# A fourth U buffer, transposes ahead of the broadcasts, and the reciprocals' small DMAs on GpSimd's queue, in a fused attention and MoE kernel

## The chip, the cores and the metric

One core of one Trainium2 chip. The metric is device time in microseconds (us). Executions are called fast or slow (a slow one is over 1.5% above the fastest of the same kernel); times below are medians of all runs, and ratios use fast runs alone.

## The reference

```python
# attention: B=8, H=12, S=448, D=64; cap = 30
scores = cap * np.tanh(scale * (q @ k.T) / cap)
attn   = np.exp(scores - max);  attn = attn / (sum(attn) + 1e-09)
out    = attn @ v
# MoE on x = out as (3584, 768); w1, w2: 768 x 1024, w_out: 1024 x 768
g = np.maximum(x @ w1, x @ w2)
y = g @ w_out
```

## The kernel before

Two heads make a pair, two pairs a quad; there are 24 quads, t = 0 to 23, and three pairs make a group g whose k, q and v are loaded together. TensorE computes scores, ScalarE tanh and exp. `pv` multiplies with v and gives U, not yet normalized, and the row sums. A small chain then fetches the reciprocals: the sums are gathered from 4 partitions by a DMA of 7 KB, inverted on VectorE, stored to DRAM (7 KB) and broadcast from there to 64 partitions twice (224 KB each). GpSimd multiplies U by it (`normalize`) into xT, and one MoE block per three quads consumes xT. MoE matmuls are strewn between the attention's, `F(n)` of them at a time, in a fixed order.

```python
def pv(t, ab):
    ...
    if ab == 0:
        U[t] = upool.tile([P, 2, S], f32, name="u", bufs=3)
    nc.vector.tensor_copy(U[t][:, ab, :], ps[:, :S])
    if ab:
        st = upool.tile([P, S], f32, name="st", bufs=1)
        nc.vector.tensor_copy(st, ss[:, :S])
        sums[t] = xpool.tile([32, 56], f32, name="sums")
        nc.sync.dma_start(out=sums[t], in_=st. ...)          # 7 KB
def invert(t):
    nc.vector.reciprocal(r, sums[t])
    nc.sync.dma_start(out=recd[t], in_=r)                    # rec_d, in DRAM, 7 KB
def spread(t):
    for h in range(2):
        nc.sync.dma_start(out=rec[t][64*h : 64*h+64], in_=...to_broadcast(...))   # rec_b
def normalize(t, ab, eng=nc.gpsimd):
    eng.tensor_mul(xT..., U[t][:, ab, :], rec[t][:, ab, :])
...
for t in range(NQ):
    scores(t + 1, 0); ex(t, 3); ...
    if t > 4:
        spread(t - 2)
    extra(i)            # loads, casts on GpSimd, cross(g): crossbar transposes
    ...
    pv(t, 0); ...
    if t > 4:
        normalize(t - 2, 0); normalize(t - 2, 1)
    scores(t + 1, 2); ...
    if t > 4:
        invert(t - 1)
    elif t > 1:
        spread(t - 2)
    extra(i + 1); ...
    pv(t, 1); ...       # ends with the sums' DMA
    if 0 < t < 5:
        invert(t - 1)
    if 1 < t < 5:
        normalize(t - 2, 0); normalize(t - 2, 1)
```

Each engine works through its own list in order; a wait in that list holds everything behind it (the 5.60 us for which VectorE stands in the prediction's first timeline are such a case).

## Time and profile before

| | before |
|---|---|
| time, median of the first 3 runs | 378.1 us (377.25 to 382.38) |
| the profiled execution | 380.94 us, span 379.2 us |
| TensorE, ScalarE, VectorE, GpSimd busy | 92%, 74%, 53%, 40% |

### The profile page before, as it was taken

How to read it: one execution, taken by the hardware profiler on the slowest of the kernel's cores; microseconds unless marked ns; L12 is line 12 of the kernel's file. 1: busy time of each engine (PE TensorE's matmuls, PEld its weight loads, DVE VectorE, ACT ScalarE, POOL GpSimd, SP SyncE). 2: the span in 40 equal slices, each digit the busy share in tenths (PEclk: the TensorE clock that was granted, in tenths of full speed). 3: DMA queues.
4: the chain of work that ended last, by engine and by line, in shares of the span. 5: the costliest groups of instructions: out<-in, count | busy, mean ns of one | idle time of the engine just before them, and what ended most of it. 6: DMA issues, size and time to landing. Idle time of an engine off the chain costs nothing.

```text
span 379.2 us, 6549 instructions
## 1 busy us (share of the span) xinstructions
PE 349.0 (92%) x2492; PEld 168.2 (44%) x2492; DVE 200.6 (53%) x348; ACT 281.8 (74%) x265; POOL 150.1 (40%) x188
## 2 busy tenths in 40 slices
PE   3677986898999999999999999999989999999996
PEld 2223443443444444444444454434434444555563
DVE  4223473567665676455745654557448556633421
ACT  4999986697999989998898899889958897000000
POOL 3734135637554445444562456243644302420000
PEclk9997898999999999999999999999989999999999
DMA  7999999996788987999698959896988132422022
GB/s 251 263 209 220 274 284 223 227 193 139 215 212 221 213 232 203 223 234 255 177 213 208 251 163 250 232 242 165 216 217 213 51 91 105 122 80 95 2 83 84
DMA packets 104464, 71.56 MB, mean 189 GB/s; under 512 B 58224, under 2 KB 99440, under 8 KB 104432
## 3 DMA queue, kind: packets, MB, share of 16 engines
q1 hardware_dynamic: 102480, 67.99, 71.1%
q0 software_dynamic: 1952, 3.15, 4.5%
q8 instruction: 19, 0.31, 0.4%
q14 instruction: 13, 0.11, 0.1%
HBM read 53.48 MB, written 11.18 MB: 171 GB/s over the span
## 4 chain that ended last, share of the span: by engine, by line
PE 65%; DMA 19%; DVE 5%; SPq 4%; ACT 3%; issue 2%; POOL 1%; POOLq 0%; DVEq 0%; ACTq 0%
PE mm L396 17%; PE mm L411 16%; PE mm L408 12%; PE pv L334 6%; DMA qkT<-kqf 6%; PE s L295 6%; DMA qr<-in_q_dram 6%; DMA vr<-in_v_dram 4%; DMA rec_b<-rec_d 3%; PE pv L348 3%; PE ss L347 2%; PE s L290 1%; DVE u L351 1%; ACT expo L303 1%; ACT tanh L296 1%
## 5 line engine op out<-in xcount | busy, mean ns | idle before, releaser
L296 ACT ACTIVATE tanh<-s 128x896 bf16<-128x896 f32 x144 | 124.3, 915 | 32.5 <-PE s L295 31.1
L303 ACT ACTIVATE expo<-tanh 128x1792 bf16<-128x1792 bf16 (+1 forms) x96 | 144.9, 1510 | 0.1
L383 POOL TENSOR_TENSOR xT<-u,rec_b 128x448 bf16<-128x448 f32 x48 | 58.4, 1238 | 101.1 <-DMA rec_b<-rec_d 81.2
L411 PE MATMUL mm<-wo_sb,gT 128*128 128x384 bf16 x448 | 86.8, 330 | 0.0
L396 PE MATMUL mm<-xT,wd_sb 128*128 128x448 bf16 x384 | 79.1, 354 | 2.7 <-POOL xT L383 1.3
L351 DVE COPY u<-pv 128x448 f32<-128x448 f32 x48 | 29.9, 624 | 91.0 <-PE pv L348 78.3
L408 PE MATMUL mm<-wm_sb,xT 128*128 128x384 bf16 x336 | 66.6, 326 | 0.2 <-DVE gT L400 0.2
L411 PEld LDWEIGHTS <-gT 128*128 128x128 bf16 x448 | 43.6, 99 | 31.1 <-issue 3.6
L415 DVE COPY osb<-mm 128x384 f32<-128x384 f32 x56 | 31.1, 555 | 46.3 <-PE mm L411 46.0
L396 PEld LDWEIGHTS <-wd_sb 128*128 128x128 bf16 x384 | 37.2, 98 | 38.4 <-issue 5.9
L295 PE MATMUL s<-qkT 64*128 64x448 bf16 x288 | 43.2, 371 | 11.1 <-ACT tanh L298 3.4
L400 DVE TENSOR_SCALAR gT<-mm 128x448 bf16<-128x448 f32 x64 | 39.1, 616 | 16.8 <-PE mm L396 16.6
L408 PEld LDWEIGHTS <-xT 128*128 128x128 bf16 x336 | 32.5, 98 | 23.3 <-issue 1.9
L334 PE MATMUL pv<-expo,vp 128*64 128x448 bf16 x288 | 37.5, 370 | 0.0
L158 POOL CAST vp<-vr 128x1152 bf16<-128x1152 f32 x15 | 18.0, 1201 | 46.8 <-DMA vr<-in_v_dram 43.5
L321 DVE TENSOR_TENSOR esum<-esum,expo 128x896 bf16<-128x896 bf16 x38 | 29.9, 787 | 1.5
L319 DVE TENSOR_TENSOR esum<-expo 128x896 bf16<-128x896 bf16 x38 | 26.6, 699 | 0.0
L295 PEld LDWEIGHTS <-qkT 64*128 64x128 bf16 x288 | 9.4, 95 | 36.8 <-issue 28.7
L298 ACT ACTIVATE tanh<-s 128x896 bf16<-128x896 f32 x24 | 22.0, 917 | 4.4 <-PE s L290 3.9
L334 PEld LDWEIGHTS <-vp 128*64 128x64 bf16 x288 | 12.4, 110 | 21.3 <-issue 15.2
L232 PE MATMUL mm<-wo_sb,w2T 128*128 128x384 bf16 x96 | 19.1, 334 | 1.4 <-DVE qkT L264 1.4
L178 POOL CAST kqf<-qr 128x1152 bf16<-128x1152 f32 x12 | 14.5, 1207 | 9.6 <-DMA qr<-in_q_dram 9.4
(56 smaller groups left out, 227.7 us busy)
## 6 DMA issues: line engine op xcount, KB each, us to landing
rec_b<-rec_d SPq DMA_DIRECT2D x48, 224.0 KB
kr<-in_k_dram SPq DMA_DIRECT2D x12, 576.0 KB
qr<-in_q_dram SPq DMA_DIRECT2D x12, 576.0 KB
vr<-in_v_dram SPq DMA_DIRECT2D x12, 576.0 KB
out_dram<-osb SPq DMA_DIRECT2D x17, 384.0 KB
out_dram<-osb SPq DMA_DIRECT2D x22, 192.0 KB
osb<-in_moe_w_dram SPq DMA_DIRECT2D x6, 512.0 KB
vr<-in_v_dram SPq DMA_DIRECT2D x8, 288.0 KB
```

The lines of the kernel that those rows point to most:

```text
L295: nc.tensor.matmul(s[:, h, :S], k0[r, j * P : (j + 1) * P], qTn[r, :])
L296: nc.scalar.activation(tanh[t, p][:, 2 * m : 2 * m + 2, :], s[:, :, :S], AF.Tanh, scale=scale / cap)
L303: nc.scalar.activation(expo[t, p], tanh[t, p][:, 0:n, :], AF.Exp, scale=float(cap))
L321: nc.vector.tensor_add(d, d, e_of(t, ab, 0 if ab else 2))
L334: nc.tensor.matmul(ps[r, :S], vp[g % 2][:, 2 * n + h, j, :], e_of(t, ab, j)[:, h, :], start=(j == 0), stop=False)
L351: nc.vector.tensor_copy(U[t][:, ab, :], ps[:, :S])
L383: eng.tensor_mul(xT[b // 2][:, hp, cs], U[t][:, ab, :], rec[t][:, ab, :])
L396: nc.tensor.matmul(ps[:, :S], wd_sb[:, c, f * P : (f + 1) * P], x[:, c, cs], start=(c == 0), stop=(c == KC - 1))
L400: nc.vector.tensor_relu(g[:, f, cs], ps[:, :S])
L408: nc.tensor.matmul(ps[:, : DM // 2], x[:, c, ts], wm_sb[:, c, hs], start=(c == 0), stop=False)
L411: nc.tensor.matmul(ps[:, : DM // 2], g[:, f, ts], wo_sb[:, f, hs], start=False, stop=(f == FC - 1))
L415: nc.vector.tensor_copy(osb[:, hs], ps[:, : DM // 2])
```

## The change

The intent: close the first hole with a fourth U buffer and by loading group 4 later; close the second by issuing the transposes ahead of the broadcast; and keep the small DMAs from standing in line with loads and stores.

```diff
+    def line(t):
+        return nc.sync if t < 3 else nc.gpsimd
...
-            U[t] = upool.tile([P, 2, S], f32, name="u", bufs=3)
+            U[t] = upool.tile([P, 2, S], f32, name="u", bufs=4)
...
-            nc.sync.dma_start(            # sums; the same edit for rec_d and rec_b
+            line(t).dma_start(
...
+            first = g == NT
+            crosses[(e - 4) // 2] = g
-            at(e - 8, load, g, "k")       # and q, and their casts
+            at(e - 8 + first, load, g, "k")
-            at(e - 4, cross, g)
...
+        if t in crosses:
+            cross(crosses[t])
         if t > 4:
             spread(t - 2)
```

More of the change, by code (lines that the diff above doesn't have):

```diff
@@ L364, in invert @@
         recd[t] = dram.tile([32, 56], f32, name="rec_d")
-        nc.sync.dma_start(out=recd[t], in_=r)
+        line(t).dma_start(out=recd[t], in_=r)
     def spread(t):
@@ L370, in spread @@
         for h in range(2):
-            nc.sync.dma_start(
+            line(t).dma_start(
                 out=rec[t][64 * h : 64 * h + 64, :, :], in_=lines[h : h + 1, :, :].to_broadcast([64, 2, S])
@@ L450 @@
     todo = [[] for _ in range(N)]
+    crosses = {}
     def at(i, f, *a):
@@ L465 @@
             e = 3 * g - g % 2
-            at(e - 8, load, g, "k")
-            at(e - 8 + g % 2, load, g, "q")
-            at(e - 6, cast, nc.gpsimd, g, "k")
-            at(e - 6, cast, nc.gpsimd, g, "q")
-            at(e - 4, cross, g)
+            first = g == NT
+            crosses[(e - 4) // 2] = g
+            at(e - 8 + first, load, g, "k")
+            at(e - 8 + max(first, g % 2), load, g, "q")
+            at(e - 6 + first, cast, nc.gpsimd, g, "k")
+            at(e - 6 + first, cast, nc.gpsimd, g, "q")
             at(e - 4, load, g, "v")
```

## The prediction

> **What bounds the kernel now.** I read the page first: busy shares, then the 40 slices, to see whether one engine bounds the whole span.
>
> ```profile
> PE 349.0 (92%) x2492; PEld 168.2 (44%) x2492; DVE 200.6 (53%) x348; ACT 281.8 (74%) x265; POOL 150.1 (40%) x188
> ...
> PE   3677986898999999999999999999989999999996
> ...
> ACT  4999986697999989998898899889958897000000
> POOL 3734135637554445444562456243644302420000
> ```
>
> TensorE is the bound, in three stages: a start to about 90 us with holes (one slice is 9.48 us), a middle to about 320 us in which ScalarE is nearly full too, and a tail of pure TensorE work. The instruction order on TensorE is fixed, so a hole that is filled moves everything after it forward; time is won only where TensorE stands still or runs slowly. So I asked for TensorE's idle time in stretches of 10 us and then finer around the two worst. Columns: stretch, its length, busy us of PE, PEld, DVE, ACT, POOL, then granted clock, DMA share, GB/s.
>
> ```profile
> 60.00:70.00 10.00, 6.34 (x71) 3.49 (x70) 3.59 (x6) 5.70 (x6) 8.15 (x10) 0.83 0.93 202
> ...
> 250.00:260.00 10.00, 9.86 (x59) 4.54 (x58) 7.18 (x12) 8.22 (x9) 4.89 (x8) 1.00 0.81 239
> ...
> 270.00:280.00 10.00, 8.15 (x54) 3.82 (x52) 5.64 (x9) 7.61 (x9) 4.53 (x4) 0.95 1.15 219
> ```
>
> ```profile
> 61.00:64.50 3.50, 0.03 (x2) 0.02 (x2) 1.17 (x3) 2.69 (x3) 3.42 (x4) 0.93 0.85 151
> 64.50:67.50 3.00, 3.00 (x38) 2.12 (x37) 2.38 (x3) 0.00 (x0) 2.88 (x4) 0.51 0.92 238
> ...
> 277.60:282.00 4.40, 4.39 (x19) 2.07 (x20) 0.77 (x2) 3.31 (x3) 1.87 (x4) 0.66 0.72 235
> ```
>
> The two holes are each followed by 3 to 4 us of reduced clock, in which PE looks fully busy but does half to two thirds of the work. Everywhere else from 90 to 320 us the idle time is tenths.
>
> The timeline says what each hole waited for. The first (time, duration, engine, line, operation; idle before it and releaser in brackets):
>
> ```profile
> 61.08 2.22 POOL L383 TENSOR_TENSOR xT<-u,rec_b 128x448 bf16<-128x448 f32 x2 [7.60 <-DMA rec_b<-rec_d]
> ...
> 63.33 0.62 DVE L351 COPY u<-pv 128x448 f32<-128x448 f32 x1 [5.60 <-POOL xT L383]
> ...
> 64.47 0.90 PE L262 MATMUL mm<-ident,kqf 64*64 64x64 bf16 x26 [3.66 <-DVE wm_sb L237]
> ```
>
> Quad 3's first U copy needs the U buffer of quad 0 (three buffers), which GpSimd frees only after normalizing, and that waited for the broadcast reciprocals, landing 9.5 us after their issue at 51.45 us, behind four loads of 576 to 672 KB in the same queue. VectorE stood for 5.60 us with the PSUM evictions behind it, and TensorE starved for 3.66 us. The second:
>
> ```profile
> 268.10 1.26 SPq L371 DMA_DIRECT2D rec_b<-rec_d  x2
> ...
> 269.47 6.05 SPq L268 DMA_TRANSPOSE qkT<-kqf  x1
> ...
> 277.61 0.55 PE L295 MATMUL s<-qkT 64*128 64x448 bf16 x4 [1.85 <-DMA qkT<-kqf]
> ```
>
> The crossbar transpose was issued behind the broadcast. SyncE had finished its previous issue at 266.64 us and then stood until 268.10. Over the run SyncE loses this to that small chain:
>
> ```profile
> SPq L371 <- DMA rec_d<-rec_s: 31.4, 14, 4.4
> ```
>
> **What the Trainium skill says.** "DMA: Bandwidth & Descriptors", section "Queues, rings and completion order": a DMA engine takes the queues that have work in turn, packet by packet. A small transfer on a second queue therefore doesn't stand behind the loads of the first. The 9.5 us of the first broadcast agree with the harmful half (one queue, in order); no trace here shows two queues with small transfers yet. The same page, "Issuing engines are not separate DMA queues": spreading over issuers adds no bandwidth, so I book no faster loads as such. "TensorE: Matmul & The Clock Gate", Part 1: the clock falls to half after an idle window of about 3.4 us and returns after a busy one. The trace agrees roughly: 0.51 after the hole of 3.66 us, but also 0.66 after one of only 1.85 us. "SBUF — State Buffer", "Who interferes with whom": VectorE in a 2-port mode can starve GpSimd's descriptor writing; VectorE's copies here mostly read PSUM and its adds are tensor_tensor, which the page thinks harmless for descriptors, so I charge little.
>
> **The change part by part.**
>
> *Fourth U buffer, and the loads of head group 4 one half-step later.* Quad 3 no longer waits for quad 0's normalize, and the first broadcast is issued ahead of four loads (k and q of group 4, some 1.3 MB). This removes the first hole: 3.66 us idle plus the slow clock, 3.00 x (1 - 0.51) = 1.5 us, together 5.1 us. Not all will stay: DMA is at a share of 0.9 to 1.1 from 10 to 80 us, so data for quads 4 and 5 can't come 5 us sooner, and the first MoE block, which already waited 1.26 us for the normalized quad 2, will wait longer. That broadcast still goes by SyncE. I keep 3.0 us (1 to 5).
>
> *Transposes ahead of the broadcast, small DMAs off SyncE.* The transpose for group 14 can be issued at about 266.7 instead of 269.47, 2.8 us sooner, against a hole of 1.85 us. [...] What can it win? The tanh after each quad's 128-row scores (L298) marks a quad. From its starts (244.72, 258.45, 270.65, 286.82, 300.61, 312.80 us) the quads take 13.73, 12.20, 16.17, 13.79, 12.19 us; a quiet set of three earlier (starts 193.74, 206.76, 219.75, 231.95) takes 13.02, 12.99, 12.20. So 16.17 + 13.79 against 26.0 is 4.0 us too long: 1.85 us hole, 4.4 x (1 - 0.66) = 1.5 us clock, 0.5 us L396 behind VectorE. The set of 244.72 has 0.5 us more of the same kind. I book 4.3 us.
>
> *What GpSimd takes on.* From quad 3, 21 x 4 = 84 DMA issues. The weight loads that it issues already show the price: four in 2.17 us, 0.54 each. So 2.2 us per quad of about 12.6, 46 us over the run, and busy POOL goes from 40% to about 52% if issues were counted. In order on one engine, a quad is then: reciprocal store 0.5, sums 0.5, wait for the store to land (about 2 us, partly under the sums), two broadcasts 1.1, casts of k and q 3.6 and of v 1.9 where both fall in one quad, normalize 2.4 to 3.0. The fullest quad sums to about 12.3 us, just one quad's length; the others to 7 to 10.4. It fits, and where it slips, the fourth U buffer and a transpose issued a quad ahead take up some microseconds. I charge 0.5 us for VectorE adds stretched by a busier GpSimd (a 128x896 add takes 0.62 alone and 1.08 us beside it) and for slips.
>
> *Added and removed work on TensorE, ScalarE, VectorE:* none. The issues removed from SyncE were not on the path by themselves.
>
> Sum: 378.1 - 3.0 - 4.3 + 0.5 = 371.3 us; I lean slightly lower, to 370.8, because single waits of tenths (the transposes' 6.2 us of TensorE and load waits in total, overlapping) shrink as well. That is 1.9% less.
>
> **Rivals.**
>
> 1. *GpSimd becomes the wait.* Its queue now holds the round trip to HBM in line with the casts that feed the transposes. For: the fullest quad has no slack; POOL already waits 43.5 us for v loads, in order. Against: casts lie a quad ahead of the transposes, and the fourth buffer. If casts come 4 us late in every third quad, each even head group's transposes stall TensorE by 1 to 2 us, with reduced clock after it: about 5 to 10 us given back, 376 to 381 us.
>
> 2. *The start is bound by DMA.* The hole at 61 us closes but reopens at 80 to 90 us before the first MoE block. For: DMA share near 1.0 there. Against: share 0.48 from 80 to 90 us, so the backlog is nearly worked off, and the hole itself had only 151 GB/s. Then only the 4.3 us remain, near 373.5.
>
> 3. *All holes close,* including those at 72 us (1.45 us behind VectorE) and 88 us: 378.1 - 5.1 - 4.8 - 2 = 366.
>
> **Range and chances.** Central 370.8; rival 3 sets the low end at 366, the DMA rival and a little of the GpSimd one the high end at 376. The line for faster by over 2% is 370.5, almost at my centre: 0.46 faster, 0.49 within 2%, 0.05 slower, since a loss needs GpSimd to add over 15 us and nothing sums to that.
>
> **What would show it.** Right: no VectorE wait of microseconds for a U buffer; TensorE idle near 61 us gone, clock 1.0 there; transposes of even head groups landing before their scores; the SyncE wait for rec_d gone and found on GpSimd's queue; quads of 13.0, 13.0, 12.2 us throughout. Wrong: TensorE waiting for qkT still or longer, released by late GpSimd casts; VectorE's reciprocals waiting for the sums; idle from 80 to 90 us grown by what 61 us lost; issues on GpSimd of well over 0.54 us.

## The result, and the profile after

The changed kernel took 395.25 us (393.32 to 399.06, 4 runs) against 379.8 us (4 runs). The ratio is 1.0419, 95% interval 1.0295 to 1.0543: 4% slower, far outside the range. (A ratio is the mean time of one kernel's fast runs over that of the other's in the same rounds, so it isn't quite the ratio of the medians.)

In the changed kernel's program the lines of the second half lie four further down: normalize is L387 (L383 before), the first MoE matmul L400 (L396), the broadcast L375 (L371). Its page, the same rows as before:

```profile
PE 355.1 (90%) x2492; PEld 168.5 (43%) x2492; DVE 211.1 (53%) x348; ACT 281.7 (71%) x265; POOL 205.4 (52%) x272
...
PE   3678898779997999999995999999987999999996
...
ACT  4999989657999589998984689988986798000000
POOL 2832363952586449663577447833966564450000
```

GpSimd's busy share is the 52% that I had forecast. Two of the prediction's stretches of 10 us, with two more, show the old holes closed and others open:

```profile
60.00:70.00 10.00, 8.45 (x114) 4.30 (x113) 6.69 (x11) 9.37 (x9) 4.53 (x6) 1.00 1.04 238
...
120.00:130.00 10.00, 7.06 (x47) 3.00 (x46) 4.93 (x8) 7.59 (x8) 8.15 (x11) 1.00 0.75 209
...
210.00:220.00 10.00, 7.06 (x26) 2.37 (x26) 1.78 (x3) 3.31 (x3) 7.12 (x11) 0.66 0.79 177
...
270.00:280.00 10.00, 10.00 (x67) 4.97 (x66) 5.43 (x11) 9.10 (x10) 5.10 (x7) 1.00 0.77 218
```

From 60 to 70 us TensorE is busy 8.45 us instead of 6.34, the clock full; 270 to 280 us is clean. But 120 to 130 and 210 to 220 us are now holes. In the kernel before they were quiet:

```profile
120.00:130.00 10.00, 10.00 (x66) 4.53 (x63) 5.28 (x9) 9.77 (x10) 2.31 (x4) 1.00 0.82 212
...
210.00:220.00 10.00, 10.00 (x67) 4.61 (x64) 5.98 (x12) 8.95 (x10) 4.38 (x7) 1.00 0.89 248
```

The waits of the changed kernel name the cause (engine, line, what it waited for, us in total, times, longest), and the timeline the worst one:

```profile
POOL rec_b L375 <- DMA rec_d<-rec_s: 52.7, 18, 5.3
POOL xT L387 <- DMA rec_b<-rec_d: 46.3, 16, 7.0
...
PE mm L400 <- POOL xT L387: 12.5, 8, 3.9
```

```profile
211.21 2.21 POOL L387 TENSOR_TENSOR xT<-u,rec_b 128x448 bf16<-128x448 f32 x2 [0.35 <-DMA rec_b<-rec_d]
...
212.39 0.53 PE L400 MATMUL mm<-xT,wd_sb 128*128 128x448 bf16 x1 [3.92 <-POOL xT L387]
```

The MoE block stands for 3.92 us until GpSimd has normalized. Before, TensorE waited for xT once:

```profile
PE mm L396 <- POOL xT L383: 1.3, 1, 1.3
```

The wait of SyncE for rec_d has moved to GpSimd, and there it is followed by the wait for the broadcast. One round on GpSimd, from its timeline in the changed kernel:

```profile
98.22 2.22 POOL L387 TENSOR_TENSOR xT<-u,rec_b 128x448 bf16<-128x448 f32 x2 [6.99 <-DMA rec_b<-rec_d]
100.39 0.55 POOL L369 DMA_DIRECT2D rec_d<-rec_s  x1
...
105.49 1.20 POOL L375 DMA_DIRECT2D rec_b<-rec_d  x2 [3.92 <-DMA rec_d<-rec_s]
...
112.99 2.86 POOL L387 TENSOR_TENSOR xT<-u,rec_b 128x448 bf16<-128x448 f32 x2
```

Read it as a ring. The store of quad t-1 stands behind the normalize of quad t-2 in GpSimd's list; the broadcast waits for the store; the next normalize waits for the broadcast, or for the casts placed between. Normalize 2.2 us, then 5.1 us until the broadcast's issue, then 7.5 us until the next normalize: 14.8 us. From 98.22 to 297.12 us there are 14 such rounds, 14.2 us each. What ends a round differs: here the casts fill the last 6.2 us; the round from 127.03 to 142.26 us holds only the casts of v, but its normalize waits 5.33 us for the broadcast. The three rounds after 297.12 us, with no casts of k and q left and the last with no cast at all, take 10.8, 11.0 and 9.1 us. So the ring is longer than a quad where it is shared with the casts and the loads. In the kernel before, the store went by SyncE and wasn't behind normalize: no ring.

To compare traces I use the 24 marks of the prediction, the starts of L298, mark t belonging to quad t's scores. Mark 5 to 6 holds the first MoE block's start; after mark 23 there is only the tail. One traced execution each, us from the start of the span:

| kernel | mark 5 | mark 6 | mark 23 | end |
|---|---|---|---|---|
| before | 79.46 | 93.91 | 312.80 | 379.2 |
| changed | 74.49 | 94.72 | 328.07 | 395.3 |
| e1 | 75.04 | 92.96 | 312.41 | 379.6 |
| e2 | 76.71 | 91.76 | 326.71 | 394.1 |
| e4 | 73.98 | 93.05 | 309.18 | 376.3 |
| e5 | 74.81 | 92.06 | 309.98 | 377.1 |
| e6 | 73.85 | 92.05 | 309.43 | 376.2 |
| e7 | 78.68 | 95.17 | 313.13 | 379.5 |
| e8 | 74.62 | 89.59 | 309.13 | 376.3 |
| e9 | 74.10 | 88.99 | 311.09 | 378.2 |
| e10 | 74.40 | 91.92 | 309.06 | 375.4 |

The changed kernel is 5.0 us ahead at mark 5, which is the first hole, and 0.8 us behind at mark 6. Between marks 6 and 23 it takes 233.4 us against 218.9: 14.5 of the 16.1 us of the loss. (Single traces: two executions of one kernel can differ by some us, as the runs of the kernel before do, 377.25 to 382.38 us. Only differences that several traces repeat are worth much.)

### The profile page after: what moved, and what is told of

The parts are those of the page before. It is cut to its first block, busy times and chain, and to the rows that moved or that the text cites. A ratio compares the mean times of both kernels' runs of the same rounds, so it can differ in the third digit from the quotient of the medians.

```text
span 395.3 us, 6506 instructions
## 1 busy us (share of the span) xinstructions
PE 355.1 (90%) x2492; PEld 168.5 (43%) x2492; DVE 211.1 (53%) x348; ACT 281.7 (71%) x265; POOL 205.4 (52%) x272
## 4 chain that ended last, share of the span: by engine, by line
PE 33%; DMA 30%; POOL 19%; issue 7%; ACT 5%; DVE 3%; SPq 1%; POOLq 0%; DVEq 0%; ACTq 0%
DMA rec_b<-rec_d 17%; DMA rec_d<-rec_s 10%; PE mm L400 10%; POOL xT L387 8%; PE mm L415 8%; PE mm L412 6%; POOL kqf L178 3%; PE s L295 3%; ACT expo L303 3%; PE pv L338 3%; ACT tanh L296 2%; POOL vl L163 2%; DMA vr<-in_v_dram 2%; DMA qr<-in_q_dram 2%; POOL rec_b L375 2%
## 5 line engine op out<-in xcount | busy, mean ns | idle before, releaser
L400 PE MATMUL mm<-xT,wd_sb 128*128 128x448 bf16 x384 | 82.4, 360 | 15.5 <-POOL xT L387 12.5
L415 PE MATMUL mm<-wo_sb,gT 128*128 128x384 bf16 x448 | 85.5, 326 | 0.0
L387 POOL TENSOR_TENSOR xT<-u,rec_b 128x448 bf16<-128x448 f32 x48 | 58.3, 1234 | 46.6 <-DMA rec_b<-rec_d 46.3
L400 PEld LDWEIGHTS <-wd_sb 128*128 128x128 bf16 x384 | 37.7, 99 | 53.3 <-issue 21.3
L375 POOL DMA_DIRECT2D rec_b<-rec_d x42 | 25.2, 601 | 56.4 <-DMA rec_d<-rec_s 52.7
L295 PE MATMUL s<-qkT 64*128 64x448 bf16 x288 | 44.8, 381 | 10.8 <-ACT tanh L296 3.2
L338 PE MATMUL pv<-expo,vp 128*64 128x448 bf16 x288 | 39.7, 387 | 0.0
L321 DVE TENSOR_TENSOR esum<-esum,expo 128x896 bf16<-128x896 bf16 x38 | 35.5, 935 | 1.5
L298 ACT ACTIVATE tanh<-s 128x896 bf16<-128x896 f32 x24 | 22.0, 916 | 11.7 <-PE s L290 11.2
L319 DVE TENSOR_TENSOR esum<-expo 128x896 bf16<-128x896 bf16 x38 | 30.1, 792 | 0.0
```

Of the source, the lines that this page charges most:

```text
L295: nc.tensor.matmul(s[:, h, :S], k0[r, j * P : (j + 1) * P], qTn[r, :])
L321: nc.vector.tensor_add(d, d, e_of(t, ab, 0 if ab else 2))
L338: nc.tensor.matmul(ps[r, :S], vp[g % 2][:, 2 * n + h, j, :], e_of(t, ab, j)[:, h, :], start=(j == 0), stop=False)
L375: line(t).dma_start(out=rec[t][64 * h : 64 * h + 64, :, :], in_=lines[h : h + 1, :, :].to_broadcast([64, 2, S]))
L387: eng.tensor_mul(xT[b // 2][:, hp, cs], U[t][:, ab, :], rec[t][:, ab, :])
L400: nc.tensor.matmul(ps[:, :S], wd_sb[:, c, f * P : (f + 1) * P], x[:, c, cs], start=(c == 0), stop=(c == KC - 1))
```

## The experiments

Theory A: the ring on GpSimd is the loss. Rival B: DMAs issued by GpSimd are slow in themselves. Rival C: the transposes ahead or the later loads do the harm. The first four kernels tell them apart; the rest ask why the expected gain didn't come even without the ring.

| kernel | median us | runs | ratio to before, 95% interval |
|---|---|---|---|
| changed | 395.25 | 4 | 1.0419 (1.0295 to 1.0543) |
| e1 rest on SyncE | 380.27 | 4 | 1.0086 (0.9977 to 1.0195) |
| e2 queue alone | 396.03 | 4 | 1.0517 (1.0395 to 1.0638) |
| e3 broadcast on SyncE | 386.51 | 4 | 1.0235 (1.0071 to 1.04) |
| e4 invert first | 380.12 | 4 | 1.0073 (0.9944 to 1.0202) |
| e5 start too | 380.86 | 6 | 1.0052 (0.9998 to 1.0107) |
| e6 fourth U alone | 379.3 | 4 | 1.0026 (0.9966 to 1.0086) |
| e7 transposes ahead alone | 382.11 | 4 | 1.0066 (0.9993 to 1.014) |
| e8 same on SyncE | 377.84 | 6 | 0.9993 (0.9942 to 1.0045) |
| e9 queue from quad 5 | 381.6 | 6 | 1.0089 (1.0032 to 1.0147) |
| e10 short normalize | 376.01 | 6 | 0.991 (0.9871 to 0.9949) |

The kernel before had 379.77 us beside e1 to e4, 378.17 beside e5 to e8 and 379.09 beside e9 and e10.

### e1: the other two parts without the queue

```diff
-        return nc.sync if t < 3 else nc.gpsimd
+        return nc.sync
```

> The change without its third part: fourth U buffer, later loads of group 4 and transposes ahead are kept, all small DMAs stay on SyncE. Theory A (the small DMAs on GpSimd form a loop: normalize of one quad, store of the next quad's reciprocals, its landing waited for in line, broadcast, its landing, next normalize, 13 to 15 us per quad against 12.5 of the compute) and rival B (transfers issued by GpSimd are slow in themselves) both expect 369 to 375 us here, the gain I had predicted. Rival C (the loss is in the transposes ahead or the later loads) expects 388 us or more.

380.27 us, ratio 1.0086. C falls: without the queue the loss is gone. But A's and B's number is missed too, because the gain isn't there. This run shows where it stayed: TensorE waits for xT 4.1 us in 4 waits, and for gT 3.4 us in 4.

### e2: the queue alone

```diff
-            U[t] = upool.tile([P, 2, S], f32, name="u", bufs=4)
+            U[t] = upool.tile([P, 2, S], f32, name="u", bufs=3)
-            crosses[(e - 4) // 2] = g
+            at(e - 4, cross, g)           # and the loads back to e - 8
```

> Only the third part: small DMAs from quad 3 on by GpSimd's queue, with three U buffers and the old places of loads and transposes. A and B: 393 to 405 us, at or above the changed kernel, since normalize lags and there is one U buffer less. C: at most 384 us.

396.03 us, ratio 1.0517. The queue alone makes the whole loss, and in the same place: marks 6 to 23 lie 235.0 us apart.

### e3: the broadcast back to SyncE

```diff
-            line(t).dma_start(
+            nc.sync.dma_start(            # rec_b only
                 out=rec[t]...
```

> The changed kernel, but the broadcasts go back to SyncE; sums and reciprocal stores stay on GpSimd's queue. A: GpSimd no longer waits in line for the store to land (52.7 us in 18 waits in the changed kernel), the loop is cut, 371 to 380 us; the wait for rec_d appears on SyncE instead. B: half of the small transfers are still slow ones, so the loss is about halved, 384 to 390 us.

386.51 us, ratio 1.0235. A's number is missed and B's is met. Looking again, I had misread my own ring: it isn't cut here. The store still stands behind normalize on GpSimd, and the broadcast behind the store; only the casts no longer wait with them. So e3 doesn't decide between A and B.

### e4: the same DMAs on the same queue, another order

```diff
         if t > 4:
+            invert(t - 1)
             normalize(t - 2, 0)
             normalize(t - 2, 1)
...
-        if t > 4:
-            invert(t - 1)
-        elif t > 1:
+        if 1 < t < 5:
             spread(t - 2)
```

> The changed kernel with one order changed: from quad 5 on the reciprocal of quad t-1 and its store are placed ahead of the normalize of quad t-2, half a quad earlier. The same transfers on the same queue, as many instructions. A: the store lands under the normalize, GpSimd's wait for rec_d falls from 52.7 us to under 15, MoE's wait for xT goes, 369 to 378 us. B: nothing changes in the transfers, 390 us or more.

380.12 us, ratio 1.0073, against 1.0419 for the changed kernel; the intervals don't overlap. This decides for A: number, kind and issuer of the transfers are the changed kernel's, and a store of GpSimd took 3.8 us from issue to landing, no less than the changed kernel's 3.5. The waits and a round on GpSimd in e4:

```profile
POOL sums L361 <- DVE st L358: 34.6, 15, 4.1
POOL rec_d L369 <- DVE rec_s L367: 34.0, 16, 4.7
...
POOL rec_b L375 <- DMA rec_d<-rec_s: 3.7, 3, 2.6
```

```profile
169.40 0.52 POOL L369 DMA_DIRECT2D rec_d<-rec_s  x1 [2.82 <-DVE rec_s L367]
...
171.16 2.23 POOL L387 TENSOR_TENSOR xT<-u,rec_b 128x448 bf16<-128x448 f32 x2 [1.24 <-DMA rec_b<-rec_d]
...
174.57 0.64 POOL L361 DMA_DIRECT2D sums<-st  x1 [1.19 <-DVE st L358]
175.50 1.19 POOL L375 DMA_DIRECT2D rec_b<-rec_d  x2 [0.29 <-DMA rec_d<-rec_s]
```

The wait for the store fell from 52.7 to 3.7 us, as it now lands under normalize. GpSimd's long waits are for VectorE, that is, for the pace of the quads: it has time left over, so it isn't the bound. But nothing is gained against the kernel before either.

### e5 and e8: the start mended, with the queue and without

```diff
+        if t == 4:
+            spread(t - 2)
         if t in crosses:
             cross(crosses[t])
...
         if t > 4:
             invert(t - 1)
+        if t > 3:
             normalize(t - 2, 0)
             normalize(t - 2, 1)
```

(The late copies of both lose t = 4.) e5 is e4 with this; e8 has also `return nc.sync` in `line`.

> The kernel of e4, and in quad 4 only: the broadcast of quad 2 is issued by SyncE ahead of the transposes of group 4 instead of behind them and the loads of v, and its normalize is placed half a quad earlier. Theory: what closed at 61 us reopened because the first MoE block waited for quad 2's normalize (quads 3 and 4 took 13.5 and 19.1 us in e4); with this it should take 13.5 and 14 to 16 us, MoE's wait for xT there gone, 372 to 377 us, below both kernels. Rival: the start is bound by the DMA's bytes, then the wait only moves to a load or a transpose and the time stays at 378 to 381.

> The kernel of e5 with all small DMAs on SyncE: what is GpSimd's queue itself worth once the order is right? If a separate queue helps as the change meant, this is 1 to 2% slower than e5, 376 to 382 us, with waits for the broadcast longer than e5's. If only the order counts, it is within 0.5% of e5.

e5: 380.86 us, ratio 1.0052, a miss: the number is that of the rival (the DMA's bytes), but its wait isn't there, since TensorE's waits from 60 to 97 us are all for VectorE and none for a load or a transpose. e8: 377.84 us, 0.9993, near the low end of its first reading in us, but it is the faster of the two, by about 0.6%, which neither reading had. The long wait for xT at the start is gone in both (e8 has 1.1 us of it left, in two waits). In e5 another one stands a little earlier. From its timeline:

```profile
73.33 2.23 POOL L387 TENSOR_TENSOR xT<-u,rec_b 128x448 bf16<-128x448 f32 x2
...
73.78 3.95 DVE L214 TENSOR_TENSOR wd_sb<-osb,gT 128x1024 bf16<-128x1024 f32 x1
...
78.26 1.12 PE L232 MATMUL mm<-wo_sb,w2T 128*128 128x384 bf16 x3 [2.57 <-DVE wm_sb L237]
```

A subtract on VectorE that takes 1.15 us elsewhere in this trace took 3.95 us, begun 0.45 us into a normalize on GpSimd and ending in the casts after it. The PSUM copy behind it came late and TensorE stood for 2.57 us, and the granted clock was 0.60 from 78.3 to 82.0 us. That the normalize held the subtract up is read from their order in this one trace; no run tested it at this place. In e8 mark 6 is reached at 89.59 us, 4.3 us ahead of the kernel before: the first hole's gain, kept this far (e9's trace agrees with 88.99 us; e10's, with the same start, has 91.92 after a wait of 2.8 us for transposes). At mark 23 e8's trace is 3.7 us ahead and at the end 2.9, but the traced execution of the kernel before was 2.8 us above its median, and the timed runs are equal. Between marks 6 and 23 e8 takes 219.5 us, no less than the 218.9 of the kernel before with its second hole. There its adds on VectorE are longer (62.4 us in all over the run, against 56.5), and so is TensorE's wait for gT in the first MoE matmuls (2.5 us at L400, against 0.7 at L396).

### e6: the fourth U buffer alone

```diff
-            U[t] = upool.tile([P, 2, S], f32, name="u", bufs=3)
+            U[t] = upool.tile([P, 2, S], f32, name="u", bufs=4)
```

> The kernel before with a fourth U buffer and nothing else. My booked gain for the first hole was 3.0 us, with the late loads. If a wait simply takes its place (the first MoE block at 85 us), 377 to 380 us, ratio 0.995 to 1.005; if the hole was really worth its 5.1 us, 373 to 375.

379.3 us, ratio 1.0026: no gain. The trace shows the exchange. Mark 5 comes at 73.85 instead of 79.46 us, 5.6 us earlier (the traces with three buffers, before, e2 and e7, have it at 76.71 to 79.46 us; those with four at 73.85 to 75.04, e3 left out), and then:

```profile
83.31 2.21 POOL L383 TENSOR_TENSOR xT<-u,rec_b 128x448 bf16<-128x448 f32 x2 [4.61 <-DMA rec_b<-rec_d]
...
84.49 0.35 PE L396 MATMUL mm<-xT,wd_sb 128*128 128x448 bf16 x1 [3.23 <-POOL xT L383]
```

The first MoE block, which had waited 1.26 us at 88.21, waits 3.23 us here, and mark 6 is only 1.9 us earlier. A second point: this kernel's transposes have their old place, yet its marks 20 to 21 lie 13.21 us apart where the kernel before had 16.17. So the hole at 275 us isn't a fixed feature of that order.

### e7: the transposes ahead alone

```diff
-            at(e - 4, cross, g)
+            crosses[(e - 4) // 2] = g
...
+        if t in crosses:
+            cross(crosses[t])
         if t > 4:
             spread(t - 2)
```

> The kernel before with the transposes issued ahead of the broadcasts and nothing else. My booked gain was 4.3 us. If the broadcast, now behind 4.4 us of transpose issue, makes normalize late instead, 378 to 384 us, with VectorE waiting for U buffers (there are three) or TensorE for xT; if not, 374 to 376.

382.11 us, ratio 1.0066. The number is that of the first reading. TensorE's wait for the transposes is no longer among its longest, and waits for wm_sb (1.9 us, 2 times) and xT (1.5 us, 2 times) stand before L396; the wait for xT is hardly longer than the 1.3 us of the kernel before, so the late normalize of that reading isn't shown. The interval includes 1, so it is no gain rather than a shown loss.

### e9: the queue from quad 5 on

```diff
-        return nc.sync if t < 3 else nc.gpsimd    # on e5
+        return nc.sync if t < 5 else nc.gpsimd
```

> The kernel of e5 with GpSimd's queue used only from quad 5 on instead of 3. The traces of e8 (quad 5 reached at 89.6 us against 92.1 in e5) and e4 (quads 5 to 23 in 216.1 us against 219.5 in e8) suggest the best of both: 374 to 377 us, ratio 0.985 to 0.995. If GpSimd's queue is worth nothing even with the order right, it is within 0.5% of e8, 377 to 380.

381.6 us, ratio 1.0089: a miss of both readings, and my sum of the best stretches of two traces was no forecast. Mark 6 came as early as hoped (88.99 us), the stretch after it took 222.1 us, with TensorE waiting 4.3 us for gT behind VectorE and 3.3 us for transposes. No gain from GpSimd's queue is shown even with the order right: e8 without it has the lower ratio (from another set of rounds, and the intervals overlap), and e5, in e8's rounds, is slower than e8.

### e10: a shorter normalize, wrong result on purpose

```diff
-        eng.tensor_mul(xT[...], U[t][:, ab, :], rec[t][:, ab, :])
+        eng.tensor_copy(xT[...], rec[t][:, ab, :])        # on e8
```

> The kernel of e8 with a wrong result on purpose: normalize on GpSimd copies the broadcast instead of multiplying U by it, so it reads one operand and should take less than half of its 1.24 us; all waits on the broadcast stay. If GpSimd's hold of SBUF against VectorE's two-input adds (77 adds and subtracts of 0.6 to 1.6 us, mean 0.77 to 0.87 against 0.62 alone) is what keeps the expected gain away, the adds fall to 0.62 to 0.70, TensorE's waits for gT and wm_sb shrink, and the time falls 2 to 5 us, ratio to before 0.987 to 0.995. If not, 0.995 to 1.003.

376.01 us, ratio 0.991 (0.9871 to 0.9949), within the range, the only kernel clearly faster than before; its result is wrong, as meant. (The count of adds and subtracts is 82, not the 77 that I wrote, and normalize shrank to 0.67 us, not to less than half.) VectorE's adds in e8, then in e10 (last columns: busy us, mean ns):

```profile
L321 DVE TENSOR_TENSOR esum<-esum,expo 128x896 bf16<-128x896 bf16 x38 | 33.2, 872 | 1.5
...
L319 DVE TENSOR_TENSOR esum<-expo 128x896 bf16<-128x896 bf16 x38 | 29.2, 767 | 0.0
```

```profile
L321 DVE TENSOR_TENSOR esum<-esum,expo 128x896 bf16<-128x896 bf16 x38 | 27.9, 734 | 1.5
...
L319 DVE TENSOR_TENSOR esum<-expo 128x896 bf16<-128x896 bf16 x38 | 24.7, 649 | 0.0
```

The adds shrank by 9.8 us though nothing was changed on VectorE, and TensorE's wait for gT from 2.5 to 1.4 us. So part of what holds the gain back is probably GpSimd and VectorE getting in each other's way. It isn't a clean proof: a shorter normalize also ends sooner, it no longer reads U, so that U's buffers come free earlier, and the intervals of e8 and e10, from different rounds, just overlap (0.9942 and 0.9949).

## Why the prediction was wrong

*What GpSimd takes on: the step that failed.* "It fits, and where it slips, the fourth U buffer and a transpose issued a quad ahead take up some microseconds." The price of an issue was right (broadcasts 0.60 us, stores and sums 0.55 to 0.64), and so was the 52%. Wrong was the sum of "about 12.3". The store's landing was put at about 2 us; it took a median 3.5 us, and GpSimd stood 2.9 us for it on average beyond the sums (52.7 / 18). In the full round shown above that wait was 3.9 us and the casts 6.2 instead of 5.5, which makes about 14.8 where 12.3 was forecast. The broadcast's landing, 4.7 us, wasn't in the sum at all, since I counted work and not what the work waits for; so the rounds with fewer casts, put at 7 to 10.4 us, came out as long (15.2 us from 127.03). Above all I took the quads' chains as independent. In the changed list they form a ring of 14.2 us against 12.7 us per quad in e4 ((309.18 - 93.05) / 17), and a fourth U buffer doesn't help against a ring longer than the quad: normalize falls back until the MoE block waits for it. 14 rounds of 1.5 us too much are 21 us, by estimate, where the prediction said that nothing sums to 15; the measured loss between marks 6 and 23 was 14.5. e4 shows the cause: one order changed and 15 us come back.

*Rival 1* named the engine, but let the harm come through late casts and transposes (376 to 381 us). It came through xT, and was 395.

*The first hole, 5.1 us of which I kept 3.0.* The hole closed as predicted, 5.0 us at mark 5. The remainder kept was nought: in e6 alone mark 6 is 1.9 us earlier and the time unchanged. I had named the wait for the first MoE block as the reason for the cut and cut too little. Against the DMA's bytes as the reason speaks e8: it moves the same bytes as e1, and reached mark 6 3.4 us before it with a broadcast, a normalize and a reciprocal placed earlier.

*The second hole, 4.3 us.* In e7 the wait for the transposes went and others came, and nothing was gained; in the changed kernel 1.8 of its 2.3 us remained. The term was also sized from one execution, itself 2.8 us above the median; e6 had no such hole with the old order.

*Rests and contention, 0.5 us.* Under-sized. In the changed kernel the 76 adds took 65.6 us against 56.5 before (35.5 + 30.1 against 29.9 + 26.6), and e10 suggests that what there is of it in e8 (62.4 us, 52.6 with the short normalize) is worth some 0.8%.

*Clock.* Right in kind: 0.66 in the stretch of the worst new hole.

What stays open: why e8, without any of the old holes in its trace, isn't faster than the kernel before in the timed runs. VectorE behind GpSimd is probably one part, by e10; how large the rest is, and how far the traced execution of before was unlike its timed ones, isn't settled. No correct version beat the kernel before clearly.

## What to carry to other kernels

Before moving a chain of dependent DMAs to an engine's queue, write out that engine's list and look for a ring: an item that waits for a landing, behind an item that waits for the last one. Add the landings, not just the issue times, and compare the ring with the period of the loop; if it is longer, change the order before anything else. And price a hole from several executions, asking which wait comes next when it closes: here each hole that a part of the change closed was followed by another wait.

## What the Trainium skill lacked or had wrong

- "DMA: Bandwidth & Descriptors", "Anatomy of one DMA — SWDGE (gpsimd) path": it says that a semaphore wait happens on the issuing sequencer before dispatch, which is just what hurt here (52.7 us on GpSimd). Its fit of 2.0 us plus bytes / 436e3 gives, by estimate, about 2.0 us for a store of 7 KB; in the changed kernel the median from issue to landing was 3.5 us.
- The same page, "Queues, rings and completion order", says that a DMA engine takes the queues in turn. It isn't wrong, but was read too far: the shorter landing on a second queue was the prediction's conclusion from it and not the page's. Broadcasts on GpSimd's queue landed in a median 4.7 us in the changed kernel; on SyncE's in e3, whose trace is slow, in 3.8. No gain from the second queue is shown.
- "SBUF — State Buffer", "Who interferes with whom": right that a VectorE instruction with two SBUF inputs meets GpSimd's reads. It lacks that several GpSimd instructions in a row can hold one off: a subtract of 1.15 us took 3.95 us beside two multiplies and the casts after them (e5).
- "TensorE: Matmul & The Clock Gate", Part 1, asks for an idle window of about 3.4 us before the clock falls. In the kernel before a hole of 1.85 us was followed by 4.4 us at 0.66.
- No page warns of the ring that a chain of dependent DMAs makes on one engine's in-order queue: 14.2 us per round here against 12.7 us per quad in e4.
